# The start of a fused attention and mixture kernel: transfers asked for before tables are built, masks by a running sum, casts queued behind copies

## The chip, the cores and the metric

The kernel runs on one core of one Trainium2 chip. The metric is the device time in microseconds (µs).

Names used below: PE is TensorE, PEld its weight loads, DVE is VectorE, ACT is the scalar engine, POOL is GpSimd. SP only starts transfers in this kernel. Its transfers are called those of the *hardware queue*, those started by GpSimd those of the *software queue*: the profile of the kernel before lists the two queues apart (17.70 and 17.31 MB), and from 8 to 13 µs, when six of the seven transfers that start are GpSimd's, it counts 0.71 MB in the software queue and 0.01 MB in the other. In this kernel only GpSimd's transfers have an fp32 source and a bf16 target; SP's first rows land as fp32 and are cast on chip (0.35 µs for the first q cast, 0.62 µs for the first k cast).

## The reference

```python
# attention: B=4, H=8, S=768, D=64; each query sees its last 128 keys and the first 4 ("sinks")
scores = (q @ k.T) / sqrt(D)
keep   = is_sink | ((rel >= 0) & (rel < window))
a      = softmax(where(keep, scores, -1e9));  attn = a @ v
# mixture: N=3072 tokens, D=512, E=4, F=1024
x = attn.transpose(0, 2, 1, 3).reshape(B * S, H * D)
p = domain_probs / (domain_probs.sum(-1) + 1e-9)
out = sum_e p[:, e] * (relu(x @ w1[e]) @ w2[e])
```

## The kernel before

The order of the instructions on every engine is decided while the kernel is built, by a list scheduler with model clocks (`t[...]`, `landed`). An operation that needs only DVE or ACT is put in a list by `later(engine, ready, slack, run)` and placed by `flush`. When nothing real is ready, the scheduler gives PE *fillers*, products on a tile of zeros (`idle_products`).

The first 256 tokens of q and k come by SP as fp32 in two halves of four heads and are cast on chip, q by DVE and k by ACT. Nearly everything else (vx, later q and k rows, weights) comes by GpSimd's software queue.

```python
t = {"pe": 1200.0, "act": 0.0, "dve": 0.0, "pool": 3350.0, "sp": 800.0, "sw": 6100.0, "hw": 0.0}
...
def cast_first(half):                      # casts of one half of the first rows, placed at once
    hs = slice(4 * half, 4 * half + 4)
    cast_at[half] = max(dve(512, landed["first", half]), act(512, landed["first", half]))
    for name in "qk":
        copy("act" if name == "k" else "dve", first[name][:, :, hs, :],
             nat[0, half, name, "raw"].rearrange("p h (t d) -> p t h d", t=2))
...
ident = consts.tile([P, P], BF16, name="ident")          # set-up, in this order
nc.vector.memset(identf, 1.0)
for sgn in (1, -1):                                      # identity: 2 selects on GpSimd
    nc.gpsimd.affine_select(out=identf, in_=identf, ...)
nc.vector.tensor_copy(out=ident, in_=identf)
...
nc.vector.memset(mask0, 1.0)
sel_own(mask0, 0); sel_prev(mask0, P); sel_own(mask0, 2 * P)   # 3 selects on GpSimd
load_v(0, (0, 1))                                        # first software-queue requests
for tb in (2, 3):
    load_nat(0, tb)                                      # q and k rows of the second group
load_w1(0, 2)                                            # first expert's w1, in two halves
nc.vector.memset(mask1, 1.0)
...                                                      # 4 selects on GpSimd
load_v(0, (2, 3))
load_w2(0)
...
def transposes(b, g, hp):                  # one head pair: q and k turned on PE, copied to qkT
    if (b, g, hp) == (0, 0, 0):
        cast_first(0)
    ...                                    # 4 transposes; the copies tr -> qkT go into `later`
    if (b, g, hp) == (0, 0, 1):
        cast_first(1)                      # so these casts stand ahead of the copies
```

The softmax here doesn't subtract the row's maximum and nothing guards it: scores larger than these inputs give would overflow.

Of the kernel before, what the change touches and what calls it, by code (L numbers as in the profile page):

```python
# [9 lines left out]
ALU = mybir.AluOpType  # L10
AX = mybir.AxisListType
FP32 = mybir.dt.float32
BF16 = mybir.dt.bfloat16
# [3 lines left out]
def kernel(  # L17
# [12 lines left out]
    nc = tc.nc  # L30

    B, H, S, D = q.shape
    NSINK = int(n_sink)
# [4 lines left out]
    P = 128  # L38
# [26 lines left out]
    DX = D + 1  # L65
# [1 line left out]



    t = {"pe": 1200.0, "act": 0.0, "dve": 0.0, "pool": 3350.0, "sp": 800.0, "sw": 6100.0, "hw": 0.0}  # L70
    ring, whole = [0.0] * 6, [False] * 6
    WARM = 6600.0
    FLIP, LATE = 300, 2500
# [7 lines left out]
    def act(cols, *deps):  # L81
        at = max([t["act"], *deps])
        t["act"] = at + 75 + cols / 1.2
        return at + 205 + cols / 1.2

    def dve(cols, *deps, rate=0.96, fixed=157):
        at = max([t["dve"], *deps])
        t["dve"] = at + fixed - 85 + cols / rate
        return at + fixed + 35 + cols / rate

    def pool(cols, *deps, fixed=190):
        at = max([t["pool"], *deps])
        t["pool"] = at + fixed + cols * 1.8
        return t["pool"] + 35
# [19 lines left out]
    def later(engine, ready, slack, run):  # L114

        pend.append((ready, ready + slack, engine, run))
# [22 lines left out]
    def join(n, done):  # L139

        got = []

        def part(at):
            got.append(at)
            if len(got) == n:
                done(max(got))
        return part

    def clock(engine, cols, rate=0.96, fixed=157):
        return act(cols) if engine == "act" else dve(cols, rate=rate, fixed=fixed)  # L150

    landed = {}
# [13 lines left out]
    consts = ctx.enter_context(tc.tile_pool(name="consts", bufs=1))  # L166
# [12 lines left out]
    nat = {}  # L179
# [26 lines left out]
    def load_first():  # L206

        raw = {name: mo.tile([P, 2, 4, 2 * D], FP32, name=f"{name}raw", tag=f"wide{i}", bufs=1) for i, name in enumerate("qk")}
        for half in range(2):
            hs = slice(4 * half, 4 * half + 4)  # L210
            for name, src in (("q", q), ("k", k)):
                x = raw[name][:, half]
                nc.sync.dma_start(
                    out=x, in_=src[0, hs, 0:G, :].rearrange("h (p t) d -> p h (t d)", t=2),
                )
                nat[0, half, name, "raw"] = x
            landed["first", half] = (4700.0, 6600.0)[half]
            t["sp"] += 1060

    def copy(engine, out, in_):  # L220
        (nc.scalar.copy if engine == "act" else nc.vector.tensor_copy)(out=out, in_=in_)

    first = {name: sb.tile([P, 2, H, D], BF16, name="qkn", tag="qkn", bufs=NQB) for name in "qk"}
    qkn_free[-2:] = [1e12] * 2
    cast_at = {}

    def cast_first(half):
        hs = slice(4 * half, 4 * half + 4)
        cast_at[half] = max(dve(512, landed["first", half]), act(512, landed["first", half]))
        for name in "qk":  # L230
            copy(
                "act" if name == "k" else "dve", first[name][:, :, hs, :],
                nat[0, half, name, "raw"].rearrange("p h (t d) -> p t h d", t=2),
            )

    def rows_at(b, g):
        return max(landed.get(("qk", b, tb), 1e12) for tb in (2 * g, 2 * g + 1))

    vx = [consts.tile([P, H, DP], BF16, name=f"vx{tb}") for tb in range(NQB)]

    def load_v(b, ts):
        for tb in ts:
            nc.gpsimd.dma_start(  # L243
                out=vx[tb][:, :, 0:D],
                in_=v[b, :, tb * P:(tb + 1) * P, :].rearrange("h p d -> p h d"),
            )
            lands(("v", b, tb), H * P, D, values_at[b - 1, min(NG - 1, (tb + 1) // 2)] if b else 0.0)
# [14 lines left out]
    def load_w2(e):  # L262
        w2_sb[e] = wpool.tile([P, NFB, Dout], BF16, name=f"w2_{e}", tag=f"w2_{e}")
        nc.gpsimd.dma_start(out=w2_sb[e], in_=moe_w2[e].rearrange("(fb p) d -> p fb d", p=P))
        lands(("w2", e), F, Dout)
# [82 lines left out]
    identf = scratch[:, 9 * P:10 * P]  # L348
# [33 lines left out]


    held = consts.tile([P, 2], BF16, name="held")
    zeros = wpool.tile([P, 2 * G], BF16, name="zeros", tag=f"wf_{E - 2}")
    nc.vector.memset(zeros, 0.0)
    vsf = consts.tile([P, B, DX], FP32, name="vsf")
# [2 lines left out]
    for h in range(H):  # L390
        r = 32 * (h // 2) + NSINK * (h % 2)
        nc.sync.dma_start(
            out=vsf[r:r + NSINK, :, 0:D], in_=v[:, h, 0:NSINK, :].rearrange("b j d -> j b d"),
        )
    ident = consts.tile([P, P], BF16, name="ident")
    nc.vector.memset(identf, 1.0)
    for sgn in (1, -1):
        nc.gpsimd.affine_select(
            out=identf, in_=identf, compare_op=ALU.is_ge, fill=0.0,
            base=0, pattern=[[sgn, P]], channel_multiplier=-sgn,  # L400
        )
    nc.vector.tensor_copy(out=ident, in_=identf)
    for x in vx:
        nc.vector.memset(x[:, :, D:DX], 1.0)



    mask0 = consts.tile([P, 3 * P], BF16, name="mask0")
    mask1 = consts.tile([P, 4 * P], BF16, name="mask1")

    def sel_own(m, c):
        nc.gpsimd.affine_select(
            out=m[:, c:c + P], in_=m[:, c:c + P], compare_op=ALU.is_ge, fill=0.0,
            base=0, pattern=[[1, P]], channel_multiplier=-1,
        )

    def sel_prev(m, c):
        nc.gpsimd.affine_select(
            out=m[:, c:c + P], in_=m[:, c:c + P], compare_op=ALU.is_gt, fill=0.0,
            base=0, pattern=[[-1, P]], channel_multiplier=1,  # L420
        )

    nc.vector.memset(mask0, 1.0)
    sel_own(mask0, 0)
    sel_prev(mask0, P)
    sel_own(mask0, 2 * P)

    load_v(0, (0, 1))
    for tb in (2, 3):
        load_nat(0, tb)  # L430
    load_w1(0, 2)

    nc.vector.memset(mask1, 1.0)
    for i in range(2):
        sel_prev(mask1, 2 * i * P)
        sel_own(mask1, (2 * i + 1) * P)
    t["pool"] += 1000
    load_v(0, (2, 3))
    load_w2(0)

    sel2 = consts.tile([P, NHP, 2, DX], BF16, name="sel2")
    vsd = {}
# [4 lines left out]
    for base, sgn in ((0, 1), (NSINK - 1, -1)):  # L447
        nc.gpsimd.affine_select(
            out=sel2, in_=sel2, compare_op=ALU.is_ge, fill=0.0, base=base,
            pattern=[[-32 * sgn, NHP], [-NSINK * sgn, 2], [0, DX]], channel_multiplier=sgn,  # L450
        )
    nc.vector.memset(half, 0.0)
    for ph in range(2):
        nc.vector.memset(half[64 * ph:64 * ph + 64, ph:ph + 1], 1.0)
    for x in ksd:
        nc.vector.memset(x, 0.0)
    nc.vector.memset(mask0[0:NSINK, 0:2 * P], 1.0)

    acc = [psum.tile([P, 2 * G], FP32, name=f"acc{i}", tag=f"o{i}", bufs=1) for i in range(2)]

# [10 lines left out]
    def transposes(b, g, hp):  # L471

        if b not in qkT:
            qkT[b] = sb.tile([P, 2, NHP, S], BF16, name="qkT", tag="qkT", bufs=1)
        if (b, g, hp) == (0, 0, 0):
            cast_first(0)
        ready = max(cast_at[hp // 2] if (b, g) == (0, 0) else rows_at(b, g), free_at())
        slot = pick()
        tr = bank(slot, [P, 2, 2, P], BF16, "tr")
        hs = slice(2 * hp, 2 * hp + 2)  # L480
        for i in range(2):
            for tt in range(2):
                rows = first["qk"[i]][:, tt, hs] if (b, g) == (0, 0) else nat[b, 2 * g + tt][:, i, hs]
                nc.tensor.transpose(tr[:, i, tt], rows, ident)  # L484
        done = pe(4 * P, ready, n=4)
        dst = qkT[b][:, :, hp, g * G:(g + 1) * G]
        ring[slot] = 1e12

        def copied(at):
            take(slot, at)  # L490
            turned_at[b, g, hp] = at

        if (b, g) == (0, 0):
            part = join(2, copied)
            for i, engine in enumerate(("dve", "act")):
                def run(engine, i=i):
                    copy(engine, dst[:, i].rearrange("c (p t) -> c p t", t=2), tr[:, i].rearrange("c t p -> c p t"))
                    part(clock(engine, 2 * P))
                later(engine, done, 0, run)
        else:  # L500
            def run(engine):
                copy(engine, dst, tr.rearrange("c i t p -> c i (t p)"))
                copied(clock(engine, 4 * P))
            later("any", done, 300, run)
        if (b, g, hp) == (0, 0, 1):
            cast_first(1)
        if hp == NHP - 1:
            for _ in range(2):
                qkn_free.remove(1e12)
                qkn_free.append(done)  # L510
            qkn_free.sort()
# [210 lines left out]
    class Attention:  # L722
# [17 lines left out]

        def flip_ready(self):
            _, b, g, hp = self.flips[0]
            rows = landed["first", hp // 2] + 600 if (b, g) == (0, 0) else rows_at(b, g)
            return max(rows, free_at(), scored_at.get(b - 1, 0.0))

        def options(self):
# [636 lines left out]
```

## Time and profile before

The kernel took 381.07 µs (median of three, 380.74 to 381.65). The execution that was profiled took 381.5 µs, so it is one of the slower ones.

| what | before |
|---|---|
| PE busy | 368.6 µs, 97% of the span |
| first software-queue request (vx) | 4.16 µs |
| second half of the first k rows landed | 7.60 µs |
| first product of scores | 9.03 µs |
| second half of w1_0 landed | 20.65 µs |
| vx rows of blocks 2 and 3 landed | 22.31 µs |
| w2_0 landed / first product with it | 27.37 / 27.46 µs |
| last q and k rows of batch 1's first group landed / last transpose of them | 66.68 / 67.41 µs |

All times of this kind, here and below, are counted from the span's start. A landing is the last completion that the trace records for that transfer.

First the profile's page for the kernel before: the busy time of each engine, the line of DMA business in 40 slices of 9.5 µs (tenths), and the shares by engine of the chain that ended last.

```profile
PE 368.6 (97%) x3959; PEld 299.5 (79%) x3959; DVE 271.6 (71%) x616; ACT 146.2 (39%) x383; POOL 72.9 (19%) x98
DMA  9999999940998999207296330122030021200101
PE 74%; DMA 15%; DVE 4%; POOL 3%; ACT 2%; issue 1%; DVEq 0%; ACTq 0%
```

PE is full, so it can't lose much but its idle time. Yet 15% of the chain is DMA, and the DMA engines are busy for 90% or more of each of the first eight slices. The chain of waits of the kernel before, between 0 and 80 µs, says where (start, duration, what):

```profile
13.77 13.61 DMA w<-in_moe_w_dram
...
27.66 14.81 DMA w<-in_moe_w_dram
...
43.09 23.59 DMA qkn<-in_k_dram
...
66.73 0.90 PE tr L484 x13
```

From 13.8 to 66.7 µs the chain is three transfers nose to tail (each counted from request to landing, so its time behind earlier transfers is in it). So until about 66 µs the end of the kernel hangs on the software queue's stream of transfers, and after it on PE alone.

The timeline of the kernel before in the first 28 µs (start, duration, engine, line, operation, output and input, count; in brackets the idle time before and what ended it), first POOL, then ACT, then PE:

```profile
1.83 0.65 POOL L398 TENSOR_SCALAR_AFFINE_SELECT scratch<-scratch 128x128 f32<-128x128 f32 x2 [1.31 <-DVE scratch L396]
3.41 0.29 POOL L412 TENSOR_SCALAR_AFFINE_SELECT mask<-mask 128x128 bf16<-128x128 bf16 x1 [0.93 <-DVE mask L423]
...
4.16 1.92 POOL L243 DMA_DIRECT2D vx<-in_v_dram  x2
...
7.63 0.62 ACT L221 CAST qkn<-kraw 128x512 bf16<-128x512 f32 x1 [2.34 <-DMA kraw<-in_k_dram]
...
9.03 1.31 PE L583 MATMUL sps<-qkT 64*128 64x256 bf16 x12 [0.22 <-DVE qkT L221]
...
20.70 1.05 PE L939 MATMUL hps<-xT,w 128*128 128x256 bf16 x8 [0.60 <-DMA w<-in_moe_w_dram]
...
22.36 0.25 PE L648 MATMUL od<-vx,aT 128*128 128x65 bf16 x3 [0.34 <-DMA vx<-in_v_dram]
...
27.46 1.25 PE L1226 MATMUL acc<-w,H 128*128 128x512 bf16 x5
```

GpSimd builds tables until 4.16 µs and asks for nothing before. The first scores stand behind the second k cast on ACT (7.63 µs), which waits for its rows. PE waits for w1_0 and vx and starts with w2_0 at the moment that it lands.

The windows view of the kernel before gives for each stretch the busy time of PE, PEld, DVE, ACT and POOL with counts, then the granted PE clock (the share of the full clock that PE was given: 1.00 is full, 0.50 half), a DMA share and GB/s. The DMA share adds the time of all packets over that of 16 engines, so it can pass 1.

```profile
2.00:3.00 1.00, 1.00 (x4) 0.36 (x3) 0.48 (x8) 0.09 (x1) 0.41 (x2) 1.00 0.78 211
...
4.00:5.00 1.00, 1.00 (x4) 0.30 (x2) 0.82 (x7) 0.33 (x1) 1.00 (x2) 1.00 0.70 190
...
7.00:8.00 1.00, 0.54 (x5) 0.25 (x3) 0.20 (x1) 0.37 (x1) 1.00 (x2) 1.00 1.83 117
```

At 2 to 3 µs all of the traffic is the hardware queue's, at 211 GB/s in packets of about 510 bytes on average. At 7 to 8 µs nearly all of it is the software queue's, at 117 GB/s in packets of about 130 bytes.

### The profile page before, as it was taken

What the parts mean: (1) busy time and instruction counts of PE and PEld (TensorE: products, weight loads), DVE (VectorE), ACT (ScalarE), POOL (GpSimd) and SP (SyncE); (2) the same over time, 40 slices, a digit from 0 to 9 for tenths busy, and PEclk for the clock granted to TensorE, in tenths of its full rate; (3) what the DMA queues carried; (4) which work ended last, traced back from release to release, by engine and by line L of the source; (5) the groups of instructions that cost most, each with busy time, mean ns of one, the idle gap of its engine ahead of it and who ended that gap; (6) DMA issues with size and microseconds to landing.
All of it is one profiled execution on the core that took longest, in us unless ns stands there. A gap on an engine that the chain in (4) does not pass through costs nothing.

```text
span 379.8 us, 9469 instructions
## 1 busy us (share of the span) xinstructions
PE 368.6 (97%) x3959; PEld 299.5 (79%) x3959; DVE 271.6 (71%) x616; ACT 146.2 (39%) x383; POOL 72.9 (19%) x98
## 2 busy tenths in 40 slices
PE   7889999999999999999999999999999999999995
PEld 3657766666766788888887888889999999999984
DVE  5764987746365898687598489489589497695780
ACT  3746433865556135536415455452111112121110
POOL 7965113700932083010010000000000000000000
PEclk9999999999999999999999999999999999999999
DMA  9999999940998999207296330122030021200101
GB/s 159 170 181 201 210 210 175 150 49 0 118 191 170 187 146 151 71 27 73 63 147 142 28 86 30 28 74 68 2 85 29 32 55 28 71 29 2 57 1 57
DMA packets 110807, 35.61 MB, mean 94 GB/s; under 512 B 94260, under 2 KB 106132, under 8 KB 110764
## 3 DMA queue, kind: packets, MB, share of 16 engines
q0 software_dynamic: 77520, 17.31, 51.4%
q1 hardware_dynamic: 33244, 17.70, 20.6%
q8 instruction: 31, 0.51, 0.6%
q14 instruction: 12, 0.10, 0.1%
HBM read 40.45 MB, written 6.34 MB: 123 GB/s over the span
## 4 chain that ended last, share of the span: by engine, by line
PE 74%; DMA 15%; DVE 4%; POOL 3%; ACT 2%; issue 1%; DVEq 0%; ACTq 0%
PE acc L1156 28%; PE hps L939 23%; PE cps L1016 11%; DMA w<-in_moe_w_dram 7%; DMA qkn<-in_k_dram 6%; PE acc L1226 6%; PE sps L583 3%; PE od L648 2%; DVE H L963 1%; ACT onat L687 1%; POOL vx L243 1%; POOL qkn L185 1%; DMA gates<-gate_rows 1%; ACT aT L608 1%; PE tr L484 1%
## 5 line engine op out<-in xcount | busy, mean ns | idle before, releaser
L939 PE MATMUL hps<-xT,w 128*128 128x256 bf16 x1056 | 131.4, 273 | 0.9 <-DMA w<-in_moe_w_dram 0.6
L939 PEld LDWEIGHTS <-w 128*128 128x128 bf16 x1056 | 99.4, 98 | 15.1 <-issue 1.6
L1156 PEld LDWEIGHTS <-H 128*128 128x128 bf16 x720 | 67.9, 98 | 11.2 <-issue 3.7
L608 ACT ACTIVATE aT<-sps 128x512 bf16<-128x512 f32 (+1 forms) x96 | 47.8, 569 | 33.9 <-PE sps L583 33.8
L963 DVE SCALAR_TENSOR_TENSOR H<-hps,gates 128x512 bf16<-128x512 f32 x84 | 57.2, 685 | 4.6 <-PE hps L939 3.6
L1156 PE MATMUL acc<-w,H 128*128 128x256 bf16 x432 | 56.4, 273 | 0.4 <-ACT acc L1180 0.4
L687 ACT ACTIVATE onat<-od,R 128x64 bf16<-128x64 f32 x144 | 33.2, 327 | 44.4 <-DVE R L675 44.3
L1226 PE MATMUL acc<-w,H 128*128 128x512 bf16 x192 | 45.4, 379 | 0.0
L243 POOL DMA_DIRECT2D vx<-in_v_dram x24 | 21.4, 902 | 81.8 <-PE od L648 70.7
L1156 PE MATMUL acc<-wf,H 128*128 128x256 bf16 x288 | 35.4, 273 | 0.8 <-ACT osb L1189 0.8
L602 DVE TENSOR_TENSOR aT<-aT,mask 128x1024 bf16<-128x1024 bf16 (+1 forms) x36 | 23.1, 642 | 16.7 <-ACT aT L608 16.5
L1189 ACT COPY osb<-acc 128x256 f32<-128x256 f32 x36 | 13.4, 373 | 55.0 <-PE acc L1156 54.9
L1226 PEld LDWEIGHTS <-H 128*128 128x128 bf16 x192 | 18.0, 98 | 18.3 <-issue 0.9
L1016 PEld LDWEIGHTS <-w 128*128 128x128 bf16 x480 | 30.6, 98 | 1.7 <-issue 0.8
L1035 DVE SCALAR_TENSOR_TENSOR H<-cps,gates 128x512 bf16<-128x512 f32 x45 | 30.6, 682 | 0.1
L1156 PEld LDWEIGHTS <-S 128*128 128x128 bf16 x288 | 27.7, 98 | 3.5 <-issue 0.3
L952 ACT ACTIVATE H<-hps 128x512 bf16<-128x512 f32 x35 | 21.3, 608 | 23.0 <-PE hps L939 22.9
L1044 ACT COPY cps<-cps 128x512 f32<-128x512 f32 x15 | 8.7, 582 | 44.1 <-PE cps L1016 44.1
L1016 PEld LDWEIGHTS <-vf 128*128 128x128 bf16 x360 | 22.5, 98 | 0.7 <-issue 0.2
L185 POOL DMA_DIRECT2D qkn<-in_k_dram x22 | 20.1, 912 | 10.3 <-DMA w<-in_moe_w_dram 8.5
L185 POOL DMA_DIRECT2D qkn<-in_q_dram x22 | 20.0, 908 | 9.6 <-PE od L648 4.0
L648 PE MATMUL od<-vx,aT 128*128 128x65 bf16 x352 | 20.7, 193 | 1.1 <-DVE aT L616 0.5
(92 smaller groups left out, 431.0 us busy)
## 6 DMA issues: line engine op xcount, KB each, us to landing
w<-in_moe_w_dram POOLq DMA_DIRECT2D x7, 1024.0 KB, 19.3
out_dram<-osb SPq DMA_DIRECT2D x24, 256.0 KB
gates<-gate_rows SPq DMA_DIRECT2D x36, 128.0 KB
vx<-in_v_dram POOLq DMA_DIRECT2D x24, 128.0 KB, 6.6
qkn<-in_q_dram POOLq DMA_DIRECT2D x22, 128.0 KB, 6.9
qkn<-in_k_dram POOLq DMA_DIRECT2D x22, 128.0 KB, 6.9
w<-in_moe_w_dram POOLq DMA_DIRECT2D x2, 512.0 KB, 9.0
qraw<-in_q_dram SPq DMA_DIRECT2D x2, 256.0 KB
```

The lines of the kernel that those rows point to most:

```text
L185: nc.gpsimd.dma_start(out=both[:, i], in_=src[b, :, tb * P:(tb + 1) * P, :].rearrange("h p d -> p h d"),)
L243: nc.gpsimd.dma_start(out=vx[tb][:, :, 0:D], in_=v[b, :, tb * P:(tb + 1) * P, :].rearrange("h p d -> p h d"),)
L602: nc.vector.tensor_mul(a, a, m[:, None, :].to_broadcast([P, 2, w]))
L608: nc.scalar.activation(out=a[:, ph], in_=sps[ph][:, 0:w], func=AF.Exp, scale=scale)
L648: nc.tensor.matmul(od[:, qi, ph], lhsT=a[:, ph, c:c + P], rhs=vx[kb][:, 2 * hp + ph, 0:DX], start=(g == 0 and i == 0), stop=(i == len(term ...
L687: nc.scalar.mul(o[:, qi, hp, ph * D:(ph + 1) * D], od[:, qi, ph, 0:D], R[:, qi, ph])
L939: nc.tensor.matmul(h[:, i].rearrange("p (q n) -> p q n", q=2), lhsT=w1_sb[e][:, db, fb * P:(fb + 1) * P], rhs=xT[b, g][:, :, db], start=(i ...
L963: nc.vector.scalar_tensor_tensor(out=dst, in0=h, scalar=0.0, in1=gate, op0=ALU.max, op1=ALU.mult,)
L1016: nc.tensor.matmul(y[:, f], lhsT=A[:, d, f * P:(f + 1) * P], rhs=T[:, d], start=(m in ("P1", "P5") and f == 0 and d == 0), stop=(d == 1), ...
L1035: nc.vector.scalar_tensor_tensor(out=dst, in0=src, scalar=0.0, in1=gate, op0=ALU.max, op1=ALU.mult)
L1156: nc.tensor.matmul(x, lhsT=self.operand(b, g, e, m)[:, f], rhs=forms[e][m][:, f], start=(k == 0 and f == 0 and m in ("P1", "P5")), stop=(k ...
L1226: nc.tensor.matmul(op, lhsT=H[:, fb // QF, fb % QF, s], rhs=w2_sb[e][:, fb, :], start=(fb == 0), stop=(fb == NFB - 1),)
```

## The change

Its intent is to start the software queue's stream earlier and the first scores earlier. It has three parts. (a) GpSimd asks for vx first, then builds the identity, then asks for rows and w1_0; other selects come later. (b) The masks are no longer built by seven GpSimd selects: DVE makes a lower or upper triangle as a running sum over the identity (a scan), and the rest by copies. (c) The casts of the second half of the first rows go into the list `later`, so that they can be placed behind the first copies to qkT. The model's constants were set anew to go with this.

```diff
-    t = {"pe": 1200.0, ..., "pool": 3350.0, "sp": 800.0, "sw": 6100.0, "hw": 0.0}
+    t = {"pe": 1200.0, ..., "pool": 420.0, "sp": 800.0, "sw": 4700.0, "hw": 0.0}
...
-            landed["first", half] = (4700.0, 6600.0)[half]
+            landed["first", half] = ((4700.0, 4700.0), (7000.0, 7900.0))[half]
...
     def cast_first(half):
-        cast_at[half] = max(dve(512, landed["first", half]), act(512, landed["first", half]))
-        for name in "qk":
-            copy(...)
+        part = join(2, cast)
+        for i, name in enumerate("qk"):
+            def run(engine, i=i, name=name):
+                copy(engine, ...)
+                part(clock(engine, 512))
+            later(("dve", "act")[i], landed["first", half][i], 0, run)
...
+    load_v(0, (0, 1))
     ident = consts.tile([P, P], BF16, name="ident")
     for sgn in (1, -1):
         nc.gpsimd.affine_select(out=identf, in_=identf, ...)
-    ...                                     # mask0 by three selects, then load_v(0, (0, 1))
     for tb in (2, 3):
         load_nat(0, tb)
     load_w1(0, 2)
-    ...                                     # mask1 by four selects
-    load_v(0, (2, 3))
-    load_w2(0)
+    nc.vector.tensor_copy(out=ident, in_=identf)
+    nc.vector.tensor_tensor_scan(mask0[:, 0:P], ident, ident, 0.0, ALU.add, ALU.max)
+    own = mask0[:, 0:P]
+    prev = mask0[:, P:2 * P]
+    nc.vector.tensor_scalar(out=prev, in0=own, scalar1=-1.0, scalar2=1.0, op0=ALU.mult, op1=ALU.add)
+    ...                                     # three copies make the rest of mask0 and mask1
+    nc.vector.memset(mask0[0:NSINK, 0:2 * P], 1.0)
+    cast_first(0)
+    flush(4700.0)
...                                          # sel2 by two selects, small memsets
+    cast_first(1)
+    load_v(0, (2, 3))
+    load_w2(0)
...                                          # in transposes(): both calls of cast_first go
-            rows = landed["first", hp // 2] + 600 if (b, g) == (0, 0) else rows_at(b, g)
+            rows = cast_at.get(hp // 2, 1e12) if (b, g) == (0, 0) else rows_at(b, g)
```

In the built order, all engines have the same sequence in both kernels from the first product with w2_0 on.

More of the change, by code (lines that the diff above doesn't have):

```diff
@@ L66 @@
     DP = 72
-    t = {"pe": 1200.0, "act": 0.0, "dve": 0.0, "pool": 3350.0, "sp": 800.0, "sw": 6100.0, "hw": 0.0}
+    t = {"pe": 1200.0, "act": 0.0, "dve": 0.0, "pool": 420.0, "sp": 800.0, "sw": 4700.0, "hw": 0.0}
     ring, whole = [0.0] * 6, [False] * 6
@@ L228, in cast_first, with cast @@
         hs = slice(4 * half, 4 * half + 4)
-        cast_at[half] = max(dve(512, landed["first", half]), act(512, landed["first", half]))
-        for name in "qk":
-            copy(
-                "act" if name == "k" else "dve", first[name][:, :, hs, :],
-                nat[0, half, name, "raw"].rearrange("p h (t d) -> p t h d", t=2),
-            )
+        def cast(at):
+            cast_at[half] = at
+        part = join(2, cast)
+        for i, name in enumerate("qk"):
+            def run(engine, i=i, name=name):
+                copy(
+                    engine, first[name][:, :, hs, :],
+                    nat[0, half, name, "raw"].rearrange("p h (t d) -> p t h d", t=2),
+                )
+                part(clock(engine, 512))
+            later(("dve", "act")[i], landed["first", half][i], 0, run)
     def rows_at(b, g):
@@ L384 @@
     held = consts.tile([P, 2], BF16, name="held")
+    nc.vector.memset(identf, 1.0)
     zeros = wpool.tile([P, 2 * G], BF16, name="zeros", tag=f"wf_{E - 2}")
@@ L394 @@
         )
+    load_v(0, (0, 1))
     ident = consts.tile([P, P], BF16, name="ident")
-    nc.vector.memset(identf, 1.0)
     for sgn in (1, -1):
@@ L401 @@
         )
-    nc.vector.tensor_copy(out=ident, in_=identf)
-    for x in vx:
-        nc.vector.memset(x[:, :, D:DX], 1.0)
-    mask0 = consts.tile([P, 3 * P], BF16, name="mask0")
-    mask1 = consts.tile([P, 4 * P], BF16, name="mask1")
-    def sel_own(m, c):
-        nc.gpsimd.affine_select(
-            out=m[:, c:c + P], in_=m[:, c:c + P], compare_op=ALU.is_ge, fill=0.0,
-            base=0, pattern=[[1, P]], channel_multiplier=-1,
-        )
-    def sel_prev(m, c):
-        nc.gpsimd.affine_select(
-            out=m[:, c:c + P], in_=m[:, c:c + P], compare_op=ALU.is_gt, fill=0.0,
-            base=0, pattern=[[-1, P]], channel_multiplier=1,
-        )
-    nc.vector.memset(mask0, 1.0)
-    sel_own(mask0, 0)
-    sel_prev(mask0, P)
-    sel_own(mask0, 2 * P)
-    load_v(0, (0, 1))
+        pool(0, fixed=320)
     for tb in (2, 3):
@@ L431 @@
     load_w1(0, 2)
-    nc.vector.memset(mask1, 1.0)
-    for i in range(2):
-        sel_prev(mask1, 2 * i * P)
-        sel_own(mask1, (2 * i + 1) * P)
-    t["pool"] += 1000
-    load_v(0, (2, 3))
-    load_w2(0)
+    for x in vx:
+        nc.vector.memset(x[:, :, D:DX], 1.0)
+    nc.vector.tensor_copy(out=ident, in_=identf)
+    mask0 = consts.tile([P, 3 * P], BF16, name="mask0")
+    mask1 = consts.tile([P, 4 * P], BF16, name="mask1")
+    nc.vector.tensor_tensor_scan(mask0[:, 0:P], ident, ident, 0.0, ALU.add, ALU.max)
+    own = mask0[:, 0:P]
+    prev = mask0[:, P:2 * P]
+    nc.vector.tensor_scalar(out=prev, in0=own, scalar1=-1.0, scalar2=1.0, op0=ALU.mult, op1=ALU.add)
+    for i, x in enumerate((prev, own)):
+        nc.vector.tensor_copy(
+            out=mask1.rearrange("p (n c q) -> p n c q", n=2, c=2)[:, :, i], in_=x[:, None, :].to_broadcast([P, 2, P]),
+        )
+    nc.vector.tensor_copy(out=mask0[:, 2 * P:3 * P], in_=own)
+    nc.vector.memset(mask0[0:NSINK, 0:2 * P], 1.0)
+    t["dve"] = 4600.0
+    cast_first(0)
+    flush(4700.0)
     sel2 = consts.tile([P, NHP, 2, DX], BF16, name="sel2")
@@ L451 @@
         )
+        pool(0, fixed=700)
     nc.vector.memset(half, 0.0)
@@ L456 @@
         nc.vector.memset(x, 0.0)
-    nc.vector.memset(mask0[0:NSINK, 0:2 * P], 1.0)
+    t["dve"] += 900.0
+    cast_first(1)
+    load_v(0, (2, 3))
+    load_w2(0)
     acc = [psum.tile([P, 2 * G], FP32, name=f"acc{i}", tag=f"o{i}", bufs=1) for i in range(2)]
@@ L474, in transposes @@
             qkT[b] = sb.tile([P, 2, NHP, S], BF16, name="qkT", tag="qkT", bufs=1)
-        if (b, g, hp) == (0, 0, 0):
-            cast_first(0)
         ready = max(cast_at[hp // 2] if (b, g) == (0, 0) else rows_at(b, g), free_at())
@@ L504, in transposes @@
             later("any", done, 300, run)
-        if (b, g, hp) == (0, 0, 1):
-            cast_first(1)
         if hp == NHP - 1:
```

## The prediction

> **What bounds the kernel now.** TensorE (PE) is 97% busy; by the windows view it hardly idles from 40 to 200 us. Its idle time lies before 30 us (about 5 us), where 26 more products on zeros only fill waits. Up to 66 us the limit is DMA: the slices show its engines 90% busy or more until about 75 us, and the chain of waits runs through transfers almost unbroken from 13.8 to 66.7 us (w 13.8-27.4, w 27.7-42.5, qkn 43.1-66.7). In the PE timeline, waits end with qkn at 14.49, the second half of w1_0 at 20.69, vx at 22.36; the first product with w2_0 starts at 27.46, right at its landing. So the start is a stream of software-queue transfers, and PE after it is fixed work.
>
> That stream starts late: GpSimd first builds the identity (1.83-2.48) and three masks (3.41-4.20), and asks for the first vx at 4.16 us. Until then only the sync queue's q/k rows move; the windows show 211, 318, 190, 285, 165, 117 GB/s for the microseconds from 2 to 8, and about 145 GB/s later for rows in the software queue.
>
> **What the change does.** GpSimd asks for vx at about 0.5 us, then builds the identity (0.65), then asks for the rows (0.9 us each) and w1_0. Seven mask selects of 0.25-0.3 us leave GpSimd; VectorE does a scan and copies[...] in place of memsets (0.38 + 0.48) and of those for sel2 and half (about 1 us), which now follow the first q cast: it starts near 5 us as before. The scalar engine's second k cast (7.63-8.25) no longer stands ahead of the qkT copies, so first scores should start near 7.2 instead of 9.0 us.
>
> The built order shows that from the first w2_0 product on all engines run the same sequence as before. So what the first scores gain (near 2 us) is worth only as much as DMA gains; otherwise PE waits for w1_0, vx and w2_0.
>
> **DMA's gain, an estimate.** Bytes are unchanged. About 1.1 MB of sync-queue loads at 318 GB/s need 3.5 us; between 2 and 7.6 us the engines moved them and about 0.2 MB of rows (1.3 us at 145 GB/s), so 0.8-1 us went unused[...]. I expect the stream 0.8 to 1.6 us earlier, best guess 1.3. [...]
>
> All of it reaches the end: w2_0 lands near 26.1 instead of 27.4, the first qkn of batch 1 near 65.4 instead of 66.7, and the last products shift with them.
>
> **Prediction:** 379.7 us, range 378.6 to 380.6. Faster by over 2%: 0.01; within 2%: 0.98; slower by over 2%: 0.01.
>
> **What would show it.** Right: first vx issue below 1 us; first scores near 7.2; w1_0's second half, vx and w2_0 1 to 1.5 us earlier; PE waiting more on DMA between 18 and 26 us; the same sequence shifted by that much to the end. Wrong: landings shifted by under 0.5 us (mixing costs throughput), or PE late at w2_0 because of reordered copies.
>
> **What would make it wrong.** Sync-queue rows so late that group 0 runs late; [...] or more DMA overlap than assumed, giving 2 us and more.

Passages that no trace or run supports are cut and marked: the time of the scan and the copies, a guess why mixed transfers might go faster, and two statements about queues and about VectorE and GpSimd. The sums stay as they were on record. On VectorE, the new work and the memsets that leave or move came to a first q cast near 5 µs as before; the scan and the copies then ran from 4.27 to 5.80 µs in the trace after. For DMA, the 0.8 to 1 µs that went unused came with the guess to 0.8 to 1.6 µs, with 1.3 as the best guess, and so to 379.7 µs from about 381.

## The result, and the profile after

The changed kernel took 379.56 µs (median of four, 379.34 to 380.14) against 380.9 µs (380.24 to 381.65) of the kernel before on the same chip. The ratio is 0.9966, with a 95% interval of 0.9944 to 0.9988. Every ratio in this document is of one kernel's fast runs to those of the kernel before in the same rounds, so it isn't quite the ratio of the medians; a plain ratio of the mean times agrees within 0.0005. A later repeat gave 379.94 µs and 0.9974 (0.9958 to 0.9989). So the gain is real, about 0.3%, or 1.0 to 1.3 µs. The two profiled executions differ by 2.0 µs (spans of 379.8 and 377.8 µs). That is more than the medians differ, because the profiled run of the kernel before was a slow one.

| what | before | after | repeat of after |
|---|---|---|---|
| first vx request | 4.16 | 1.31 | 1.31 |
| second half of first k rows landed | 7.60 | 8.83 | 9.48 |
| first product of scores | 9.03 | 7.83 | 8.05 |
| second half of w1_0 landed | 20.65 | 19.14 | 18.95 |
| vx of blocks 2 and 3 landed | 22.31 | 20.47 | 20.75 |
| w2_0 landed / first product | 27.37 / 27.46 | 25.47 / 25.89 | 25.73 / 26.17 |
| w1_1 landed | 37.40 | 35.96 | 36.05 |
| last rows of batch 1's first group landed | 66.68 | 65.10 | 65.17 |
| start of the last product | 376.11 | 374.16 | 374.40 |

The chain's shares by engine on the page after, against 74% PE and 15% DMA before:

```profile
PE 87%; DMA 7%; POOL 2%; ACT 2%; issue 1%; DVE 1%; POOLq 0%; ACTq 0%; DVEq 0%
```

The chain of waits of the kernel after, 0 to 80 µs:

```profile
21.17 14.80 DMA w<-in_moe_w_dram
36.01 1.05 PE hps L932 x8
...
65.05 1.00 PE tr L479 x16
```

The chain leaves DMA at 36.0 µs, where w1_1 lands (35.96), and is PE work from there. In the kernel before it left DMA at 66.7 µs. The transposes of batch 1 show which of the two waited there. The timeline of PE's weight loads in the kernel before, from 65 µs on:

```profile
66.22 0.26 PEld L484 LDWEIGHTS <-qkn 128*128 128x128 bf16 x3
66.73 0.73 PEld L484 LDWEIGHTS <-qkn 128*128 128x128 bf16 x13 [0.25 <-DMA qkn<-in_k_dram]
```

And in the kernel after:

```profile
64.94 0.93 PEld L479 LDWEIGHTS <-qkn 128*128 128x128 bf16 x14
```

Before, PE arrived and waited 0.25 µs for the k rows. After, it had no wait there. PE and the stream of transfers arrive almost together, 1.5 µs earlier than before. Counted by product number without the fillers, PE is 1.43 µs ahead at product 300 (38.60 to 37.17) and 1.58 µs ahead at product 600 (74.78 to 73.20); at the last one it is 1.95. The additional 0.36 µs comes at 204 to 206 µs, where one wait on ACT's `onat` was 0.85 µs before and 0.49 after, in the same sequence of instructions. That is scatter of one execution, not the change.

The timeline after in the first 26 µs, POOL, DVE, PE, ACT, and PE again:

```profile
1.31 1.92 POOL L250 DMA_DIRECT2D vx<-in_v_dram  x2 [0.79 <-POOLq L1357]
3.31 0.66 POOL L406 TENSOR_SCALAR_AFFINE_SELECT scratch<-scratch 128x128 f32<-128x128 f32 x2
...
5.69 1.25 POOL L185 DMA_DIRECT2D qkn<-in_q_dram  x1
...
4.01 0.23 DVE L417 CAST ident<-scratch 128x128 bf16<-128x128 f32 x1 [2.04 <-POOL scratch L406]
4.27 0.42 DVE L420 TENSOR_TENSOR_SCAN mask<-ident 128x128 bf16<-128x128 bf16 x1
...
5.24 0.56 DVE L428 COPY mask<-mask 128x128 bf16<-128x128 bf16 x1
...
6.10 0.35 DVE L221 CAST qkn<-qraw 128x512 bf16<-128x512 f32 x1
...
7.83 0.67 PE L576 MATMUL sps<-qkT 64*128 64x256 bf16 x8 [0.59 <-DVE qkT L221]
...
8.94 0.62 ACT L221 CAST qkn<-kraw 128x512 bf16<-128x512 f32 x1
...
20.51 0.25 PE L641 MATMUL od<-vx,aT 128*128 128x65 bf16 x3 [0.53 <-DMA vx<-in_v_dram]
...
25.89 1.90 PE L1219 MATMUL acc<-w,H 128*128 128x512 bf16 x8
```

The two vx requests hold GpSimd for 1.92 µs, so the identity comes only at 3.97 µs, and DVE stands idle for 2.04 µs waiting for it. After the scan and the copies its first q cast starts at 6.10 µs, a microsecond later than before (5.11). That the scores still start 1.2 µs earlier is due to part (c): ACT's second k cast now runs at 8.94 µs, behind the copies.

The windows of the kernel after, for the same stretches as above:

```profile
2.00:3.00 1.00, 1.00 (x4) 0.30 (x2) 0.00 (x0) 0.09 (x1) 1.00 (x2) 1.00 0.81 226
...
4.00:5.00 1.00, 1.00 (x4) 0.40 (x3) 0.89 (x4) 0.28 (x1) 1.00 (x2) 1.00 1.20 124
...
7.00:8.00 1.00, 0.41 (x8) 0.28 (x6) 0.82 (x8) 0.59 (x2) 1.00 (x2) 1.00 1.77 208
```

In the first 8 µs the hardware queue now moves 1.07 MB and the software queue 0.22 MB (1.12 and 0.17 MB before), and the last of the hardware queue's first k rows lands 1.2 to 1.9 µs later (7.60 to 8.83 and 9.48). Over the kernels below it is the same: with the first vx request at 1.3 µs these rows landed between 8.83 and 9.75 µs (five traces), with the request at 3.4 to 4.9 µs between 6.90 and 7.60 µs (four). By 8 µs the hardware queue had moved 1.03 to 1.07 MB in the five and 1.12 MB in the four.

One reading goes against the prediction's reasoning. By 8 µs both kernels have moved the same 1.29 MB, 0.17 MB of it in the software queue before and 0.22 MB after. The bytes differ afterwards: between 8 and 14 µs the rate is 149 GB/s before and 176 GB/s after. So the change didn't fill unused room with more bytes in the first 8 µs. It changed which queue's bytes came first, and the weights were reached earlier: w1_0 was asked for at 7.79 µs instead of 9.52.

### The profile page after: what moved, and what is told of

The parts are those of the page before. It is cut to its first block, busy times and chain, and to the rows that moved or that the text cites. A ratio compares the mean times of both kernels' runs of the same rounds, so it can differ in the third digit from the quotient of the medians.

```text
span 377.8 us, 9452 instructions
## 1 busy us (share of the span) xinstructions
PE 367.0 (97%) x3954; PEld 298.7 (79%) x3954; DVE 271.8 (72%) x619; ACT 146.6 (39%) x383; POOL 71.6 (19%) x91
## 4 chain that ended last, share of the span: by engine, by line
PE 87%; DMA 7%; POOL 2%; ACT 2%; issue 1%; DVE 1%; POOLq 0%; ACTq 0%; DVEq 0%
PE acc L1149 29%; PE hps L932 29%; PE cps L1009 12%; PE acc L1219 10%; DMA w<-in_moe_w_dram 7%; PE sps L576 3%; PE od L641 2%; POOL qkn L185 1%; POOL vx L250 1%; PE od L634 1%; ACT onat L680 1%; PE tr L479 1%; ACT aT L601 0%; PE sinks L546 0%; ACT osb L1182 0%
```

## The experiments

Twelve kernels were run, each in five rounds beside the kernel before, in three batches on three chips (the kernel before: 380.9, 380.82 and 381.01 µs, 11 runs each). All gave correct results.

Two theories stood against each other. *Stream*: the gain is the earlier start of the software queue's stream; scores that start earlier are worth nothing, since PE then waits for weights. *First scores*: the gain is PE's earlier start of real work. The experiments led to a third statement, which contains both: two chains race to about 66 µs, and the later one counts. It was made after the runs, and the kernels with delayed requests don't bear it out.

### The change repeated

> The changed kernel once more, as the base for the runs beside it. Both theories: about 1.3 to 1.6 us below the kernel before (ratio 0.9958 to 0.9968), first vx request near 1.3 us, first scores near 7.8, first product with w2_0 near 25.9.

It gave 379.94 µs, 0.9974 (0.9958 to 0.9989). Its second k rows landed at 9.48 µs rather than 8.83, and its first fillers ran at half rate (0.213 µs per 256 columns against 0.109 in the first profile). So these two readings vary from run to run.

### Casts behind copies alone

To the kernel before, only part (c) is applied; GpSimd's program is unchanged.

```diff
 # kernel before
-            landed["first", half] = (4700.0, 6600.0)[half]
+            landed["first", half] = ((4700.0, 4700.0), (6600.0, 7600.0))[half]
 ...                                  # cast_first and flip_ready as in the change
+    cast_first(0)
+    flush(4700.0)
+    cast_first(1)
     acc = [...]
```

> The kernel before with only the casts part of the change: second casts behind the first copies; GpSimd keeps its sequence, first vx request near 4.2 us. First scores near 7.3 instead of 9.0. Stream theory: w2_0 lands near 27.4 as before, ratio 0.999 to 1.001. Rival (first scores are the gain): ratio near 0.9966.

It gave 381.08 µs, 0.9999 (0.9976 to 1.0021). The first scores started at 7.05 µs, two microseconds earlier than before and earlier than in the changed kernel. But the last rows of batch 1's first group landed at 66.73 µs (66.68 before). On the way w2_0 landed at 26.75 µs, not near 27.4 as expected, although GpSimd's requests were unchanged: a landing in a single trace can lie off by 0.6 µs. The timeline of PE's weight loads shows where the lead went:

```profile
66.77 0.73 PEld L492 LDWEIGHTS <-qkn 128*128 128x128 bf16 x13 [0.76 <-DMA qkn<-in_k_dram]
```

PE came earlier and waited 0.76 µs instead of 0.25. So earlier scores alone gain nothing: the theory of the first scores falls.

### Early requests alone

To the kernel before, only the requests are moved: vx first, the rows and w1_0 ahead of the selects of mask0.

```diff
 # kernel before
+    nc.vector.memset(identf, 1.0)
+    load_v(0, (0, 1))
     zeros = wpool.tile(...)
 ...
+    for tb in (2, 3):
+        load_nat(0, tb)
+    load_w1(0, 2)
     nc.vector.memset(mask0, 1.0)
     sel_own(mask0, 0); sel_prev(mask0, P); sel_own(mask0, 2 * P)
-    load_v(0, (0, 1))
-    ...
+    nc.gpsimd.memset(mask0[0:NSINK, 0:2 * P], 1.0)
```

> The kernel before with only the order on GpSimd changed: vx, identity, rows, w1_0 are asked for before the masks. PE and ScalarE keep the sequence of the kernel before. DMA as in the changed kernel: w2_0 lands 1.5 to 1.9 us earlier (25.5 to 25.9). But the second k cast stands ahead of the copies and its rows land near 8.9, so first scores near 10.3. Stream theory with small slack: PE late at w2_0, gain of 0 to 0.7 us (ratio 0.998 to 1.0). If the early requests are all that counts: 0.9966.

It gave 382.13 µs, 1.0028 (1.0011 to 1.0044): slower than the kernel before, though the stream came as early as in the changed kernel (w2_0 landed at 25.83 µs, the rows of batch 1 at 65.27). PE was late. Timeline of ACT and PE near 10 µs, and of the weight loads near 67 µs:

```profile
9.12 0.62 ACT L221 CAST qkn<-kraw 128x512 bf16<-128x512 f32 x1 [3.80 <-DMA kraw<-in_k_dram]
...
9.79 0.82 PE L483 MATMUL tr<-ident,qkn 128*128 128x128 bf16 x6 [1.36 <-ACT qkn L221]
10.54 1.46 PE L582 MATMUL sps<-qkT 64*128 64x256 bf16 x12
...
67.57 0.99 PEld L483 LDWEIGHTS <-qkn 128*128 128x128 bf16 x16
```

The requests of the software queue delayed the second k rows to 9.09 µs (7.60 before). Their cast on ACT stands ahead of the copies to qkT, so the copies, and with them the scores, waited: 10.54 µs against 9.03. The windows show a second loss (third number from the right is the granted clock):

```profile
8.00:10.50 2.50, 1.08 (x9) 0.67 (x8) 0.55 (x3) 1.38 (x4) 2.50 (x8) 0.82 2.28 165
10.50:14.00 3.50, 3.50 (x30) 1.82 (x28) 2.99 (x9) 3.07 (x9) 3.50 (x7) 0.50 1.79 183
```

By the trace's clock records PE fell to half its clock at 9.60 µs, in the second of two gaps (1.27 and 1.36 µs), and stayed there until 16.42 µs. All six timed runs have a lowered mean clock (0.990 to 0.996), so what the casts cost and what the clock cost isn't told apart here. PE reached the first product with w2_0 at 28.95 µs, 3.1 µs after w2_0 had landed, and the transposes of batch 1 at 67.57 µs, with no wait left. So here PE is the later chain. Early requests need part (c).

### The change without part (c)

```diff
 # changed kernel, in cast_first
+        if half == 1:              # placed at once, ahead of the copies
+            cast_rows("dve", "q")
+            cast_rows("act", "k")
```

> The changed kernel with the casts of the second half directly behind those of the first on both engines, as in the kernel before; all other sequences are the same. The second k rows land near 8.9 us now, so the first qkT copies wait for them and first scores start near 10 instead of 7.8 us. DMA is unchanged: w2_0 lands near 25.5. Stream theory with PE's slack of only about 0.5 us: PE comes late to w2_0 and 0.8 to 1.5 us of the gain are lost (ratio 0.998 to 1.0). Stream theory with enough slack (fillers and waits absorb it): ratio stays near 0.9966.

Its five fast runs lie between 382.06 and 382.89 µs, 1.0037 (1.0018 to 1.0055). The profiled run fell into a slow state (477.04 µs, mean granted clock 0.751), so its trace isn't used and the mechanism isn't shown for this kernel. The time fits that of the early requests alone. One of the five ran at full clock and was the slowest (382.89 µs), so a lowered clock alone isn't what the missing part (c) costs.

### The change without part (b)

```diff
 # changed kernel; the selects follow the requests for w1_0
-    nc.vector.tensor_tensor_scan(mask0[:, 0:P], ident, ident, 0.0, ALU.add, ALU.max)
-    ...                                        # and the copies
+    nc.vector.memset(mask0, 1.0)
+    nc.vector.memset(mask1, 1.0)
+    ...                                        # seven affine_selects on GpSimd
```

> The changed kernel with the masks built by GpSimd selects again, but after its requests for the rows and w1_0 (mask0 near 9.5 to 10.3 us, mask1 to 11.5), not by the scan on VectorE. VectorE's first q cast comes about 1 us sooner, but the first mask product waits for mask0, 1.5 us later than in the changed kernel. Stream theory: DMA is unchanged up to w1_0, and the loss is what PE lacks in slack, 0 to 1 us (ratio 0.9966 to 0.999). If the scan is the gain itself: ratio near 1.

It gave 383.39 µs, 1.0058 (1.0032 to 1.0084), the slowest of all. The stream was early again (w2_0 at 26.00, the rows of batch 1 at 65.01 µs), and the scores were earlier than in any other kernel with vx asked first (6.85 µs). But the masks came late, as GpSimd was busy with requests. One line of PE's timeline, a later one with fillers, and the windows:

```profile
12.17 0.24 PE L642 MATMUL od<-vx,aT 128*128 128x65 bf16 x1 [3.55 <-DVE aT L610]
...
19.75 1.70 PE L462 MATMUL acc<-zeros 128*128 128x256 bf16 x7
```

```profile
12.00:16.00 4.00, 3.31 (x27) 1.98 (x28) 2.90 (x9) 1.78 (x5) 4.00 (x5) 0.50 1.37 201
16.00:20.00 4.00, 2.99 (x34) 2.70 (x33) 3.64 (x8) 2.05 (x5) 4.00 (x9) 0.50 1.73 185
```

PE stood idle for 3.55 µs from 8.62 µs on. By the trace's clock records it went to half clock at 11.98 µs, 3.4 µs after it had stopped, and came back at 22.22 µs: 256-column fillers followed each other every 0.213 µs (0.109 before). It came to w2_0 at 31.04 µs. The timed runs say the same: three of them with a mean granted clock of 0.987, as in this trace, took 383.94 to 384.58 µs, the three at 0.990 to 0.996 took 382.23 to 382.84 µs.

### The same with the gap filled

```diff
 # the kernel of the last section, ahead of the first product with vx
+        if (b, hp, g) == (0, 0, 0):
+            for _ in range(28):
+                nc.tensor.matmul(acc[1][:, 0:G], lhsT=zeros[:, 0:P], rhs=zeros[:, 0:G], start=True, stop=True)
```

> masks_on_gpsimd with 28 more products on zeros (about 3.05 us at full rate) in PE's gap of 3.55 us before the first values product, nothing else. In masks_on_gpsimd PE came out of that gap at half rate (0.213 us for 256 columns, against 0.109 before it) and stayed so to 20.8 us. Theory (late tables cost twice: the wait itself, and PE's fall to half rate after the gap): values still start near 12.2 us, but the fillers near 14.5 to 20 us run at 0.109, and the time falls by 1 to 2.5 us against masks_on_gpsimd (ratio 0.999 to 1.003). Rival (only the wait on the masks costs): time as masks_on_gpsimd, ratio near 1.0058.

With 28 useless products it took 381.91 µs, 1.0028 (1.0005 to 1.005) instead of 1.0058. The two were run in different batches on different chips, each against the kernel before, and their intervals overlap, so the times alone don't make it sure; the traces show what changed. The windows and one line of PE's timeline:

```profile
12.00:16.00 4.00, 3.05 (x43) 2.16 (x44) 3.41 (x11) 2.27 (x7) 4.00 (x5) 1.00 1.35 202
16.00:20.00 4.00, 2.83 (x41) 1.94 (x40) 3.93 (x10) 2.12 (x6) 4.00 (x9) 1.00 1.73 183
```

```profile
17.01 0.93 PE L462 MATMUL acc<-zeros 128*128 128x256 bf16 x7
```

The clock stays at 1.00, seven fillers take 0.93 µs instead of 1.70, and the first product with w2_0 starts at 28.55 instead of 31.04 µs. Against the changed kernel (25.89 µs) that is 2.5 of 5.2 µs, about half of PE's delay in these traces; of the loss in time, 0.0030 of 0.0084 to 0.0092, it is about a third. The rest would be the late masks themselves.

### The identity first, and requests delayed

In the first of three kernels, the identity is built ahead of the vx requests. In the other two, four or eight spare selects on GpSimd delay the requests further. PE, ACT and DVE have the same sequences in all three.

```diff
 # changed kernel
-    load_v(0, (0, 1))
     ident = consts.tile([P, P], BF16, name="ident")
     for sgn in (1, -1):
         nc.gpsimd.affine_select(out=identf, in_=identf, ...)
+    nc.gpsimd.memset(spare, 1.0)                       # not in the first of the three
+    for _ in range(4):                                 # 8 in the third
+        nc.gpsimd.affine_select(out=spare, in_=spare, ...)
+    load_v(0, (0, 1))
```

> GpSimd builds the identity before it asks for vx; nothing else moves. First vx request near 1.8 instead of 1.3 us, the row requests near 3.7 as in the changed kernel; identity ready 2 us sooner, so first scores near 6.9 instead of 7.8. Theory of the stream: w2_0 lands within 0.3 us of the changed kernel and the time is the same within 0.3 us (ratio to before near 0.9966). Rival (the gain is that the first scores start earlier): about 0.9 us faster than the changed kernel (ratio near 0.994).

> As identity_first, but GpSimd spends about 1.3 us on a memset and 4 selects of a spare tile before its first request (near 3.1 us). PE, VectorE and ScalarE keep their sequences. Theory of the stream: first product with w2_0 near 26.6 us, time about half way between the two kernels (ratio 0.998). Rival: no loss, first scores still near 6.9, ratio 0.994 to 0.9966.

> As identity_first, with a memset and 8 selects of a spare tile, so the first request goes near 4.2 us as in the kernel before, while the first scores still start near 6.9. Theory of the stream: first product with w2_0 back near 27.4 us and time that of the kernel before within 0.4 us (ratio 0.999 to 1.001). Rival: the gain stays, ratio 0.994 to 0.9966.

| first vx request | µs | ratio (95%) | w2_0 landed / used | rows of batch 1 landed |
|---|---|---|---|---|
| 1.31, the change repeated | 379.94 | 0.9974 (0.9958 to 0.9989) | 25.73 / 26.17 | 65.17 |
| 1.76, identity first | 380.46 | 0.9981 (0.9965 to 0.9998) | 24.79 / 25.52 | 64.72 |
| 3.37, half late | 379.51 | 0.9968 (0.9951 to 0.9986) | 26.45 / 27.51 | 65.28 |
| 4.87, late | 381.94 | 1.0026 (1.0009 to 1.0043) | 26.59 / 27.67 | 65.98 |

Requests at 4.87 µs take the gain away and more (0.999 to 1.001 was expected), although parts (b) and (c) are there and the first scores start at 6.63 µs. It is tempting to lay this to the stream, but the traces don't bear it out. The stream moved only 0.9 µs (1.1 against the first run of the change) at w2_0 for a request that came 3.56 µs later, since the hardware queue's rows then went ahead (second k rows at 6.90 µs instead of 9.48). By 8 µs the hardware queue had moved 1.12 MB and the software queue 0.13 MB, against 1.05 and 0.20 MB in the repeat of the change: nearly the same sum, shared otherwise. The stream landed even earlier than in the kernel before, which asked at 4.16 µs (w2_0 at 26.59 against 27.37 µs, the rows of batch 1 at 65.98 against 66.68). In the profiled run PE itself was late, as the timeline of the late kernel shows:

```profile
14.21 1.14 PE L486 MATMUL tr<-ident,qkn 128*128 128x128 bf16 x9 [0.86 <-DMA qkn<-in_k_dram]
...
16.12 1.70 PE L468 MATMUL acc<-zeros 128*128 128x256 bf16 x7
```

By the trace's clock records PE was at half clock from 11.75 to 18.58 µs (seven fillers took 1.70 µs), after a wait for vx (1.02 µs, ended at 9.89); a wait for k rows (0.86 µs, ended at 14.21) falls into it. PE used w2_0 1.1 µs after its landing. But this run (380.75 µs) was the fastest of its six, and the three runs with a mean clock of 0.998 or more took 381.98 to 382.39 µs. So neither the half clock nor the landings of this trace explain why the kernel is slower than the kernel before: that stays open.

The half-late kernel missed the expectation of a result half way between: it was as fast as the change. Its profiled run (381.0 µs) was the slowest of its six, so its trace doesn't stand for the other five. Why it loses nothing stays open. The delay also moves GpSimd's own later work (a wait of 1.47 µs on the sink keys that GpSimd makes, in its profile), so these kernels don't vary the requests alone.

The identity first makes the first scores 1.0 to 1.2 µs earlier (6.84) and most landings 0.3 to 0.9 µs earlier in its profile, but it isn't faster in the timed runs; the intervals overlap. Part of the lead is scatter: the kernel "rows before w2" below has the same requests up to w2_0, and there w2_0 landed at 25.77 µs. And four of its six runs, not the profiled one, had a lowered clock (see the end of this section). At the transposes of batch 1 PE waited 0.37 µs for the k rows there. More lead for PE ends in a wait, as with the casts alone.

### Versions meant to be better

On the kernel with the identity first, two orders of requests were changed, alone and together. The first asks for vx of blocks 2 and 3 ahead of the second half of w1_0. The second asks for batch 1's first rows ahead of the last expert's w2, to take away the wait at 65 µs.

```diff
 # kernel with the identity first
-    load_w1(0, 2)
+    load_w1(0, 2, (0,))            # first half only
 ...
     load_v(0, (2, 3))
+    load_w1(0, 2, (1,))            # second half
     load_w2(0)
```

> Towards a faster version: identity_first with the two vx transfers asked for before the second half of w1_0, on whose landing PE still waited 0.5 to 0.7 us near 20 us. If that wait is worth anything, PE comes to w2_0 0.3 to 0.6 us sooner; but then it meets the landings of w2_0, w1_1 and of the k rows of the next batch near 65 us, which do not move. Stream theory: no more than 0.3 us better than identity_first (ratio 0.996 to 0.998). Rival (PE's own start counts): 0.5 us better, ratio near 0.9955.

```diff
 # kernel with the identity first
-            loads += [(load_w1, 3), (load_w2, 3)]
-            for tb in range(NQB):
+            loads += [(load_w1, 3), (load_nat, 1, 0), (load_nat, 1, 1), (load_w2, 3), (load_v, 1, (0,)), (load_v, 1, (1,))]
+            for tb in range(2, NQB):
```

> Towards a faster version, and a test of the limit near 65 us: identity_first with the first rows of batch 1 asked for before w2_3. In identity_first PE was 0.7 us ahead of the changed kernel near 37 us, and lost 0.3 of it waiting for the k rows that landed at 64.72. Stream theory: these rows now land near 60 us, PE keeps its 0.7 us past 65 us, time 0.3 to 0.6 us under the changed kernel (ratio 0.9945 to 0.997), unless w2_3, now landing near 65 us, becomes the wait. Rival (that wait is chance): same as identity_first.

> Identity first, vx before the second half of w1_0, and rows of batch 1 before w2_3, together. If both waits (near 20 and near 65 us) are real limits, this is the fastest: 0.5 to 1.0 us under the changed kernel (ratio 0.994 to 0.996). If w2_0 and w1_1 limit PE between them, no better than identity_first_rows_before_w2.

| kernel | µs | ratio (95%) |
|---|---|---|
| values before second half of w1_0 | 380.04 | 0.9971 (0.9946 to 0.9996) |
| rows before w2 | 379.68 | 0.9967 (0.9947 to 0.9988) |
| all three | 379.25 | 0.9953 (0.9933 to 0.9974) |

With the rows first, the transposes of batch 1 ran at 59.6 to 60.6 µs with no wait for DMA, so that wait is gone; the time hardly moved. All three together gave the lowest time and beat the kernel before. Its interval overlaps that of the changed kernel (0.9958 to 0.9989 in the repeat), so it isn't shown to beat that one.

### The parts side by side

| early requests | scan | casts behind | kernel | ratio to before |
|---|---|---|---|---|
| no | no | yes | casts behind alone | 0.9999 |
| yes | no | no | early requests alone | 1.0028 |
| yes | yes | no | change without (c) | 1.0037 |
| yes | no | yes | change without (b) | 1.0058 |
| no (4.87 µs) | yes | yes | requests late | 1.0026 |
| half (3.37 µs) | yes | yes | requests half late | 0.9968 |
| yes | yes | yes | the change | 0.9966, repeat 0.9974 |

The scan alone, and the scan with the casts at the old request time, were not run. The four kernels of this table that came out slower than the kernel before were all slower than the expectations allowed (1.0 for early requests alone and for the change without (c), near 1 without (b), 1.001 for late requests).

The record gives a mean granted clock for each timed run. In three traces a mean of 0.991 goes with 6.8 µs at half clock (early requests alone, requests late, values before second half of w1_0), so it tells roughly how long a run was slowed. Sorted by it, the mean times are:

| kernel | 0.998 or more | below |
|---|---|---|
| before, the batch of the repeat | 380.95 (11 runs) | none |
| the change repeated | 379.72 (4) | 380.40 (2) |
| identity first | 379.54 (2) | 380.58 (4) |
| values before second half of w1_0 | 379.20 (2) | 380.29 (4) |
| rows before w2 | 379.46 (2) | 379.90 (4) |
| all three | 379.21 (6) | none |
| requests late | 382.24 (3) | 381.25 (3) |

At full clock the first five changed kernels lie within about 0.5 µs of each other, so much of the lead of "all three" over the identity first is that none of its runs was slowed. Why its runs weren't isn't shown. The gain of the change over the kernel before stands at full clock too. The groups are small and were sorted afterwards, and the late kernel goes the other way.

## Why the prediction was right

The predicted time of 379.7 µs was 0.14 µs off the measured 379.56, and the range held it. Point by point:

- **The limit.** "The start is a stream of software-queue transfers, and PE after it is fixed work" was right. The end moved with the landings of w1_1 (1.44 µs) and of batch 1's rows (1.58 µs).
- **Scores worth only what DMA gains.** Right, and shown: the casts alone made the first scores 2 µs earlier and gained nothing, with a wait of 0.76 µs in its place.
- **What (b) and (c) are for.** Here a step was missing. The prediction costed them as freeing GpSimd and moving the first scores. It didn't see that early requests alone are a loss of 0.28%, since they delay the rows on the other queue and PE then becomes the later chain. With (b) or (c) left out, or the requests at 4.87 µs, the gain was gone (with requests at 3.37 µs it wasn't): together they let PE and the stream arrive at the same time. It named the danger as what would make it wrong ("sync-queue rows so late that group 0 runs late"). Part (c) kept that from happening.
- **DMA's gain.** It was right in direction, but its accounting was not shown. It said that between 2 and 7.6 µs "0.8-1 us went unused". But by 8 µs both kernels had moved 1.29 MB. The lead in bytes comes between 8 and 14 µs (176 against 149 GB/s). The shift was 1.5 µs at w1_0's second half, 1.9 at w2_0 and 1.6 at batch 1's rows, against 1.3 predicted. But w2_0 is the least sure of these: in the trace of the casts alone it landed at 26.75 µs with the old requests. The extra 27 GB/s over 6 µs are about 0.16 MB, at the 186 GB/s that follow (14 to 20 µs, before) an estimated 0.9 µs, so they cover only part of the shift. Where the rest comes from isn't settled.
- **Mis-sized terms.** The first request came at 1.31 µs, not "about 0.5". The first q cast started at 6.10 µs, not "near 5", because two vx requests hold GpSimd for 1.92 µs and the identity waits behind them, which DVE needs for the scan. So the first scores started at 7.83 µs (8.05 in the repeat), not 7.2. The second k rows landed at 8.83 and 9.48 µs instead of 7.60. Up to w1_1 none of these is seen to cost time: PE's weight loads still waited 0.26 µs for its landing (35.96 µs).
- **Waits.** "PE waiting more on DMA between 18 and 26 us" was wrong. The wait there is 0.53 µs (vx) against 0.60 and 0.34 µs (w1_0 and vx) before.
- **The requests for rows.** Three of the four took 0.88 to 0.90 µs, as predicted (0.9); the one at 5.69 µs took 1.25. No run shows why.

## What to carry to other kernels

Where two chains race (here the stream of transfers and PE's own start), moving one forward pays only until the other is later, so test the parts of such a change one at a time before giving any of them the credit. A request that is made earlier can delay what was in flight already (here the second k rows, from 7.60 to 8.83 and 9.48 µs); look up who waits for *that*, and move its consumer back in the order of its engine. After a long idle time, look whether PE is slow for microseconds more (here 10.2 µs at half clock after 3.55 µs idle). It was slow after shorter gaps too: 6.8 µs at half clock with two gaps of 1.27 and 1.36 µs in the kernel with early requests alone. Filling the gap of 3.55 µs with useless products recovered about half of PE's delay in the traces and about a third of the time. And look at which of the timed runs the trace comes from: the trace of the late kernel is its fastest run, and explains nothing about the slower ones.
